# Planning the order of instructions with a transfer's issue and its bytes as two resources

## The chip, the cores and the metric
The kernel runs on one core of one Trainium2 chip. Its engines are TensorE (PE in the profile; PEld are its weight loads), VectorE (DVE), ScalarE (ACT), GpSimd (POOL) and SyncE (SP); here SP issues all transfers (DMAs). The metric is the device time of one execution in microseconds. Three runs of the kernel before took 653.82, 656.34 and 656.34 us; the median is 656.34 us.

## The reference
Causal attention over 4 batches of 12 heads (448 positions, 64 features each) gives x; a gated MLP follows. Weights arrive as 64-bit floats, and the kernel turns them into 32-bit ones.

```python
scores = scale * np.matmul(q, k.transpose(0, 1, 3, 2))
scores = np.where(mask, -1000000000.0, scores)
attn = np.exp(scores - np.max(scores, axis=-1, keepdims=True))
attn = attn / (np.sum(attn, axis=-1, keepdims=True) + 1e-09)
x = np.matmul(attn, v)               # then (batch*seq, heads*features) = (1792, 768)
gate = 1.0 / (1.0 + np.exp(-(x @ w_gate)))
out = gate * (x @ w_val) @ w_out     # w_gate, w_val: 768 x 1536; w_out: 1536 x 768
```

## The kernel before
Heads are taken in 24 pairs, six to a batch; a batch's 448 tokens are one unit of the MLP. Units 0 and 1 run the MLP as it stands (line 600: three matmuls for each product, since weights and activations are each split into a high and a low half). Units 2 and 3 are done together by a Strassen-like scheme with seven products in place of eight (line 813). First comes an opening with the attention of batch 0, up to about 45 us; then attention is mixed into the MLP of units 0 and 1: batch 1 in the narrow form, and from about 220 to 395 us batches 2 and 3 in the wide form; from 417 us on the paired units run alone.

A narrow pair loads `raw` (q and k, line 257) and `vr` (v, line 263), makes scores on TensorE, exponentials on ScalarE, scales on GpSimd, transposes on TensorE, copies to `pt`, and multiplies with v (line 358). A wide pair does the transposition differently: VectorE transposes blocks of 32 into `room`, one 1 MB transfer writes them to a buffer `pd` in device memory (line 463), four transfers of 256 KB read them back with the blocks in their new places as `pt` (line 466), and line 483 multiplies with `vr`.

A weight of units 0 and 1 is handled by `weight`. For unit 0 the 768 KB of 64-bit words go to `room` (line 565), ScalarE and VectorE build the 32-bit words in `wr` (lines 569 to 573), which are also stored to `wdram` (line 576); for unit 1 `wr` is read back from there (line 578). ScalarE then rounds to `wh` (line 581), and VectorE or GpSimd takes the rest, `wl` (line 583). There are three buffers each of `wr`, `wh` and `wl`.

The order of all this is written by no hand. Every operation is entered in a `Plan` with its engine, a cost in us, what it reads and writes, perhaps a due time, and an `extra`: time that passes after its end until another engine may use the result. `order()` first carries due times back from users to makers, then simulates the engines: the engine that can start earliest takes, among its operations ready by then, the one with the earliest due time. The starts so found give the sequence in which the instructions are emitted. Only the sequence reaches the chip: each engine then runs its own queue in that order and waits for semaphores, whatever times the plan had. SP is an engine in this plan as the others are: before the change a transfer holds it for its bytes at 355 GB/s and 0.03 us, and its result counts as there 2.8 or 4.2 us later. Three costs of the plan around the change:

```python
act = lambda n, psum=0, acc=0: n / 1200 + (0.06 if psum else 0.09) + 0.1 * acc
dma = lambda b: b / 355e3 + 0.03
LAT, LOOK, SLACK = 0.04, 0.06, 0.2
```

Of the kernel before, what the change touches and what calls it, by code (L numbers as in the profile page):

```python
# [10 lines left out]
I32 = mybir.dt.int32  # L11
# [4 lines left out]
B, H, S, D = 4, 12, 448, 64  # L16
DM, DFF = 768, 1536
KD, KF = DM // 128, DFF // 128
# [19 lines left out]
EV = ((1, 3, 4), (0, 1, 2, 3, 4), (1, 3, 4), (1, 3, 4))  # L38
BUFS = dict(w64=3, wd=2, wr=3, ws=3, sm=4, raw=3, pt=3, gt=5, vr=2, st=4)
LAT, LOOK, SLACK = 0.04, 0.06, 0.2  # L40
AFTER = dict(DVE=0.09, ACT=0.1, PL=0.03)


# [34 lines left out]


class Op:  # L80
    __slots__ = ("eng", "cost", "fn", "due", "preds", "succs", "make", "left", "ready", "n", "extra", "after", "then", "lock")


class Plan:
# [14 lines left out]
    def op(self, eng, cost, fn, reads=(), writes=(), due=None, extra=0.0, lock=False):  # L99
        o = Op()  # L100
        o.lock = lock or eng == "PL"
        o.eng, o.cost, o.fn, o.due, o.extra = eng, cost, fn, due, extra + AFTER.get(eng, 0.0)
        o.n = len(self.ops)
        preds = set()
        o.make, o.after, o.then = [], [], []
        for b, *ks in writes:
            if not b.ops:
                o.make.append(b)
                if b.before is not None:
                    preds.update(b.before.ops)  # L110
                if b.prev is not None and b.prev.ops:
                    o.after.append(b.prev.ops[0])
            else:
                o.after.append(b.ops[0])
        for b, *ks in reads:
            for k in ks or (0,):
                preds.add(b.last[k])
                b.readers.setdefault(k, []).append(o)
            b.ops.append(o)
        for b, *ks in writes:  # L120
            for k in ks or (0,):
                if k in b.last:
                    preds.add(b.last[k])
                preds.update(b.readers.get(k, ()))
                b.last[k] = o
                b.readers[k] = []
            b.ops.append(o)
        preds.discard(o)
        o.preds = preds
        o.succs = []  # L130
        o.after = [q for q in set(o.after) if q not in preds]
        for q in preds:
            q.succs.append(o)
        for q in o.after:
            q.then.append(o)
        self.ops.append(o)
        return o
# [6 lines left out]

    def order(self):
        for o in reversed(self.ops):
            d = min((s.due - s.cost - SLACK for s in o.succs), default=1e9) - o.extra
            o.due = d if o.due is None else min(o.due, d)
        free = {}
        shared = 0.0  # L150
        queue = {}
        for o in self.ops:
            o.left = len(o.preds) + len(o.after)
            o.ready = 0.0
            queue.setdefault(o.eng, [])
            free[o.eng] = 0.0
            if not o.left:
                queue[o.eng].append(o)
        done = []
        while True:  # L160
            best = None
            for e, q in queue.items():
                if q:
                    t = max(free[e], min(o.ready for o in q))
                    if best is None or t < best[0]:
                        best = (t, e)
            if best is None:
                break
            t, e = best
            q = queue[e]  # L170
            o = min((o for o in q if o.ready <= t + LOOK), key=lambda o: (o.due, o.n))
            q.remove(o)
            start = max(t, o.ready, shared if o.lock else 0.0)
            end = start + o.cost
            if o.lock:
                shared = end
            free[e] = end
            done.append((start, o.n, o))
            for s in o.succs:
                s.left -= 1  # L180
                s.ready = max(s.ready, end + o.extra + (LAT if s.eng != e or e != "PE" else 0.0))
                if not s.left:
                    queue[s.eng].append(s)
            for s in o.then:
                s.left -= 1
                s.ready = max(s.ready, start)
                if not s.left:
                    queue[s.eng].append(s)
        assert len(done) == len(self.ops)
        done.sort(key=lambda x: x[:2])  # L190
        return [o for _, _, o in done]
# [3 lines left out]
def kernel(  # L195
# [7 lines left out]
    nc = tc.nc  # L203
    plan = Plan()
# [7 lines left out]

    dve = lambda n: 0.07 + n / 960
    act = lambda n, psum=0, acc=0: n / 1200 + (0.06 if psum else 0.09) + 0.1 * acc
    dma = lambda b: b / 355e3 + 0.03

    ident = new("ident", [128, 128], F32)
    mask = new("mask", [128, 4 * WQ], F32)
# [31 lines left out]
    def load(n):  # L250
        j = pairs[n]
        j["raw"] = r = new("raw", [128, 2 * S], F32, BUFS["raw"])
        halves_ = lambda x: x.rearrange("p (y n) -> p y n", y=2)
        cols = (0, 2 * QB, S) if n == 0 else (0, S)
        for e, (a, c) in enumerate(zip(cols, cols[1:])):
            keys_ = (e,) if n == 0 else (0, 1)
            plan.op("SP", dma(128 * 2 * (c - a) * 4), lambda a=a, c=c: nc.sync.dma_start(
                out=halves_(r.t)[:, :, a:c], in_=halves_(qkt[n])[:, :, a:c]), writes=[(r, *keys_)], extra=2.8)

    def load_v(n):  # L260
        j = pairs[n]
        j["vr"] = v = new("vr", [128, NB, 2, D], F32, BUFS["vr"])
        plan.op("SP", dma(128 * NB * 2 * D * 4), lambda: nc.sync.dma_start(
            out=v.t.rearrange("p c z d -> p (c z d)"), in_=vt[n]), writes=[(v,)], extra=2.8)

    def score(n, blocks, due):

# [177 lines left out]
    def shift(n):  # L445
# [3 lines left out]
        tb = part(4 * WC, n % 2)  # L449
        tv = lambda: tb.t.rearrange("p (r n) -> p r n", r=4)  # L450
        plan.op("PL", 0.2, lambda: nc.gpsimd.memset(tv()[:, 2:4, WC - 32:WC], 0.0), [], [(tb, "zero")])
        for z, i in [(z, i) for i in range(3) for z in range(2)] + [(0, 3)]:
            sm, o, c, at = j["sm"][z], woff(i), min(i + 1, 3), z * 192 + ioff(i) if i < 3 else 384
            r = [(sm, (i, z))] if i < 3 else [(sm, (i, 0), (i, 1))]
# [6 lines left out]
            [(j["sm"][0], (3, 0), (3, 1))], [(tb, "end")])  # L461
        pd = new("pd", [128, 4 * WC], F32, 2, bass.MemoryType.DRAM)
        plan.op("SP", dma(128 * 4 * WC * 4), lambda: nc.sync.dma_start(out=pd.t, in_=tb.t),
                [(tb, "zero", "end", *[(z, i) for z in range(2) for i in range(3)], (0, 3))], [(pd,)], extra=4.2)
        for r in range(4):
            plan.op("SP", dma(32 * 4 * WC * 4), lambda r=r: nc.sync.dma_start(  # L466
                out=pt.t[32 * r:32 * r + 32, :4 * WC].rearrange("p (a n) -> p a n", a=4),
                in_=pd.t.rearrange("(a p) (r n) -> r p a n", a=4, r=4)[r]), [(pd,)], [(pt, r)], extra=4.2)

    def wpv(n, due):  # L470
        j = pairs[n]
# [82 lines left out]
    def weight(p):  # L554
# [3 lines left out]
        if p < NP:  # L558
# [4 lines left out]
            ri = lambda: t.t.rearrange("p k m -> p (k m)").bitcast(I32)  # L563
            n = KD * 128
            o = plan.op("SP", dma(128 * n * 8), lambda: nc.sync.dma_start(
                out=q.t.bitcast(I32), in_=wp[p]), [], [(q,)], extra=4.2)
            if p >= EARLY:
                plan.behind(o, pairs[min(HP - 2, 1 + p)]["r"].ops[0])
            plan.op("ACT", act(n) + 0.1, lambda: nc.scalar.activation(
# [3 lines left out]
            plan.op("DVE", 0.87, lambda: nc.vector.scalar_tensor_tensor(  # L573
                out=ri(), in0=lo(), scalar=29, in1=ri(), op0=ALU.logical_shift_right, op1=ALU.bitwise_or),
                [(q,)], [(t,)], lock=True)
            plan.op("SP", dma(128 * n * 4), lambda: nc.sync.dma_start(out=wd.t, in_=t.t), [(t,)], [(wd,)], extra=4.2)
        else:
            plan.op("SP", dma(128 * KD * 128 * 4), lambda: nc.sync.dma_start(out=t.t, in_=wd.t), [(wd,)], [(t,)], extra=4.2)
        hi_ = new("wh", [128, KD, 128], F32R, BUFS["ws"])
        lo_ = new("wl", [128, KD, 128], F32R, BUFS["ws"])  # L580
        plan.op("ACT", act(768), lambda: nc.scalar.copy(hi_.t, t.t), [(t,)], [(hi_,)])  # L581
# [6 lines left out]
    def unit_items(u):  # L588
# [44 lines left out]
        def f_out(m, half, k, due):  # L633
# [9 lines left out]
            if c == KF - 1:  # L643
                o = new("gt", [128, S], F32, BUFS["gt"])
                plan.op("ACT", act(S, 1), lambda: nc.scalar.activation(
                    out=o.t, in_=ps.t[:, :S], func=ACTF.Copy, scale=0.5), [(ps,)], [(o,)])
                plan.op("SP", dma(128 * S * 4), lambda: nc.sync.dma_start(
                    out=out[m * 128:(m + 1) * 128, u * S:(u + 1) * S], in_=o.t), [(o,)], [], due + 10.0, extra=4.2)

        order = [(jj, gv, k) for jj in range(KF) for gv in range(2) for k in range(KD)]  # L650
        if u == 0:
# [74 lines left out]
    def pair_items():  # L726
# [11 lines left out]
        def fetch(src, p=None):  # L738
            p = p or take()
            plan.op("SP", dma(128 * KD * 128 * 4), lambda: nc.sync.dma_start(  # L740
                out=p.t, in_=src.t.rearrange("p k m -> p (k m)")), [(src,)], [(p, 0, 1)], extra=4.2)
            return p

        def cut(p, lo=0, n=2, vector=False):
# [45 lines left out]
        def out_sums(m):  # L790
# [9 lines left out]
            for p, x in ("5", a22), ("7", a21), ("6", a11), ("3", a12):  # L800
                d = sums[p, m] = new(f"sum{p}{m}", [128, KD, 128], F32, 1, bass.MemoryType.DRAM)
                plan.op("SP", dma(128 * KD * 128 * 4), lambda d=d, x=x: nc.sync.dma_start(
                    out=d.t.rearrange("p k m -> p (k m)"), in_=x.t), [(x, 0, 1)], [(d,)], extra=4.2)
            sums["1", m], sums["2", m], sums["4", m] = at(m, 0), at(m, 1), at(KH + m, 1)

        sums = {}
# [35 lines left out]

        def write(src, row, u):
            plan.op("SP", dma(128 * S * 4), lambda: nc.sync.dma_start(
                out=out[row * 128:(row + 1) * 128, u * S:(u + 1) * S], in_=src.at), [src.ref], [], st["now"] + 10.0, extra=4.2)

        def stage():

# [237 lines left out]
```

## Time and profile before

| | before |
|---|---|
| runs (us) | 656.34, 653.82, 656.34 |
| profiled execution (us) | 654.04 |
| its span, first to last instruction (us) | 652.3 |
| granted TensorE clock, mean | 0.994 of full speed |
| busy us: TensorE, VectorE, ScalarE, GpSimd | 642.1, 445.5, 359.4, 323.3 |
| moved by transfers | 137.15 MB, mean 210 GB/s |

Busy time is the union of an engine's instructions; matmuls overlap, so their mean duration is longer than the distance from one start to the next. A wait is idle time of an engine, put down to what ended it. Time on SP's queue is issue time and waiting; the bytes move afterwards, and "to landing" counts from the issue to the last byte.

### The profile page before, as it was taken

How to read it: one execution, taken by the hardware profiler on the slowest of the kernel's cores; microseconds unless marked ns; L12 is line 12 of the kernel's file. 1: busy time of each engine (PE TensorE's matmuls, PEld its weight loads, DVE VectorE, ACT ScalarE, POOL GpSimd, SP SyncE). 2: the span in 40 equal slices, each digit the busy share in tenths (PEclk: the TensorE clock that was granted, in tenths of full speed). 3: DMA queues.
4: the chain of work that ended last, by engine and by line, in shares of the span. 5: the costliest groups of instructions: out<-in, count | busy, mean ns of one | idle time of the engine just before them, and what ended most of it. 6: DMA issues, size and time to landing. Idle time of an engine off the chain costs nothing.

```text
span 652.3 us, 10853 instructions
## 1 busy us (share of the span) xinstructions
PE 642.1 (98%) x3726; PEld 539.9 (83%) x3726; DVE 445.5 (68%) x999; ACT 359.4 (55%) x815; POOL 323.3 (50%) x352
## 2 busy tenths in 40 slices
PE   6999999999999999999999999999999999999997
PEld 4566887888888778778787899999999999999997
DVE  4776987878774376556565975647764459999852
ACT  6887777767664456555465645443343434556520
POOL 3751653241520277577666766756665657700300
PEclk9899999999999999999999999999999999999999
DMA  7379599877886369998989895767532322344321
GB/s 269 120 243 327 193 305 324 264 262 260 275 295 227 118 216 270 296 303 258 280 277 293 242 308 186 227 243 242 178 114 78 114 76 73 121 134 152 98 80 70
DMA packets 46678, 137.15 MB, mean 210 GB/s; under 512 B 5152, under 2 KB 8736, under 8 KB 45088
## 3 DMA queue, kind: packets, MB, share of 16 engines
q1 hardware_dynamic: 46624, 136.47, 64.0%
q8 instruction: 29, 0.48, 0.3%
q14 instruction: 25, 0.20, 0.1%
HBM read 99.48 MB, written 36.96 MB: 209 GB/s over the span
## 4 chain that ended last, share of the span: by engine, by line
PE 95%; DMA 2%; ACT 2%; SPq 0%; DVE 0%; POOL 0%; issue 0%; DVEq 0%
PE m L600 40%; PE m L813 19%; PE s L813 10%; PE t L813 7%; PE t L334 4%; PE s L283 4%; PE m L358 3%; PE m L483 3%; PE s L405 3%; DMA raw<-in_qkt_dram 2%; ACT sm L300 1%; PE t L405 1%; PE s L358 1%; POOL wl L583 0%; SPq L466 0%; ACT sm L426 0%
## 5 line engine op out<-in xcount | busy, mean ns | idle before, releaser
L767 POOL TENSOR_TENSOR wl<-room,wh 128x384 fp32r<-128x384 f32 x84 | 96.7, 1174 | 55.2 <-ACT wh L766 55.0
L600 PE MATMUL m<-xh,wh 128*128 128x448 f32 x288 | 109.8, 381 | 0.0
L600 PE MATMUL m<-xh,wl 128*128 128x448 f32 x288 | 105.3, 365 | 0.0
L600 PE MATMUL m<-xl,wh 128*128 128x448 f32 x288 | 105.2, 365 | 0.0
L583 POOL TENSOR_TENSOR wl<-wr,wh 128x768 fp32r<-128x768 f32 x38 | 74.4, 1961 | 54.0 <-ACT wh L581 53.4
L321 POOL TENSOR_SCALAR sm<-sm,r 112x112 f32<-112x112 f32 (+1 forms) x92 | 62.6, 701 | 77.4 <-DVE r L308 71.4
L581 ACT CAST wh<-wr 128x768 fp32r<-128x768 f32 x72 | 59.6, 830 | 30.7 <-PE m L600 19.6
L600 PEld LDWEIGHTS m<-xh,wh 128*128 128x128 f32 x288 | 54.1, 188 | 20.3 <-issue 13.3
L766 ACT CAST wh<-room 128x384 fp32r<-128x384 f32 x84 | 39.6, 512 | 54.2 <-POOL wl L767 15.9
L426 ACT ACTIVATE sm<-sm,mn 128x128 f32<-128x128 f32 (+3 forms) x84 | 43.9, 524 | 43.3 <-DVE mn L420 43.3
L600 PEld LDWEIGHTS m<-xh,wl 128*128 128x128 f32 x288 | 54.1, 188 | 4.5
L600 PEld LDWEIGHTS m<-xl,wh 128*128 128x128 f32 x288 | 54.2, 188 | 3.7
L300 ACT ACTIVATE sm<-sm,mn 112x112 f32<-112x112 f32 (+3 forms) x96 | 49.8, 521 | 9.8 <-DVE mn L296 9.4
L600 PE MATMUL m<-gh,wh 128*128 128x448 f32 x144 | 53.9, 374 | 0.0
L441 POOL TENSOR_SCALAR sm<-sm,r 128x256 f32<-128x256 f32 (+3 forms) x84 | 42.7, 525 | 21.7 <-DVE r L436 12.4
L583 DVE TENSOR_TENSOR wl<-wr,wh 128x768 fp32r<-128x768 f32 x34 | 36.2, 1065 | 24.2 <-ACT wh L581 23.9
L600 PE MATMUL m<-gh,wl 128*128 128x448 f32 x144 | 52.6, 366 | 0.0
L600 PE MATMUL m<-gl,wh 128*128 128x448 f32 x144 | 52.6, 365 | 0.0
L455 DVE STREAM_TRANSPOSE room<-sm 128x384 f32<-128x384 f32 (+2 forms) x84 | 35.1, 448 | 19.1 <-POOL sm L441 17.9
L630 POOL TENSOR_TENSOR gl<-gt,gh 128x448 fp32r<-128x448 f32 x24 | 30.4, 1268 | 34.2 <-ACT gh L629 34.2
L813 PE MATMUL m<-pt,wh 128*128 128x448 f32 x150 | 44.7, 366 | 0.0
L420 DVE CUSTOM_DVE_ANT_0 sm<-s,mask 128x128 f32<-128x128 f32 (+1 forms) x72 | 29.2, 440 | 21.5 <-PE s L405 20.9
(165 smaller groups left out, 1488.9 us busy)
## 6 DMA issues: line engine op xcount, KB each, us to landing
room<-in_wp_dram SPq DMA_DIRECT2D x36, 768.0 KB, 6.6
wr<-wdram SPq DMA_DIRECT2D x45, 384.0 KB, 5.0
room<-wdram SPq DMA_DIRECT2D x45, 384.0 KB, 3.6
wdram<-wr SPq DMA_DIRECT2D x36, 384.0 KB, 7.1
pd<-room SPq DMA_DIRECT2D x12, 1024.0 KB, 6.9
pt<-pd SPq DMA_DIRECT2D x48, 256.0 KB, 5.7
raw<-in_qkt_dram SPq DMA_DIRECT2D x23, 448.0 KB, 6.2
vr<-in_vt_dram SPq DMA_DIRECT2D x24, 256.0 KB, 6.1
```

The source lines that it names most:

```text
L300: plan.op("ACT", act(ne, 0, 1) + 0.01, lambda z=z, sm=sm, i=i, ne=ne, off=off: nc.scalar.activation(out=sm.t[:QB, off:off + ne], in_=sm.t[ ...
L321: plan.op("PL", 0.24 + w / 1200, lambda args=args: nc.gpsimd.tensor_scalar(**args()), [(r_,)], [(sm, a)])
L426: plan.op("ACT", act(ne, 0, 1) + 0.01, lambda z=z, sm=sm, i=i, ne=ne, off=off: nc.scalar.activation(out=sm.t[:, off:off + ne], in_=sm.t[:, ...
L441: plan.op("PL", 0.24 + w / 1200, lambda sm=sm, i=i, o=o, w=w, z=z: nc.gpsimd.tensor_scalar(out=sm.t[:, o:o + w], in0=sm.t[:, o:o + w], sca ...
L455: plan.op("DVE", dve(128 * c) + 0.03, lambda sm=sm, i=i, o=o, c=c, at=at: nc.vector.transpose(out=tv()[:, :, at:at + 32 * c].rearrange("p ...
L581: plan.op("ACT", act(768), lambda: nc.scalar.copy(hi_.t, t.t), [(t,)], [(hi_,)])
L583: plan.op(eng, cost, lambda: at.tensor_tensor(out=lo_.t, in0=t.t, in1=hi_.t.bitcast(F32), op=ALU.subtract), [(t,), (hi_,)], [(lo_,)], lock ...
L600: nc.tensor.matmul(out=ps.t[:, :S], lhsT=a.t[:, k, :], rhs=b.t if isinstance(b, Buf) else b(), start=(first and z == 0), stop=(last and z ...
L630: plan.op("PL", 1.11, lambda: nc.gpsimd.tensor_tensor(out=gl.t[:, jj], in0=gg.t, in1=gh.t.bitcast(F32), op=ALU.subtract), [(gg,), (gh,)], ...
L766: plan.op("ACT", act(w), lambda: nc.scalar.copy(f(hi_.t), x()), [(src, at)], [(hi_, e)])
L767: plan.op("PL", 0.97, lambda: nc.gpsimd.tensor_tensor(out=f(lo_.t), in0=x(), in1=f(hi_.t).bitcast(F32), op=ALU.subtract), [(src, at), (hi_ ...
L813: nc.tensor.matmul(out=ps.t[:, :S], lhsT=a.t[:, kw, :], rhs=b.at, start=bool(first and z == 0), stop=bool(last and z == 2), skip_group_che ...
```

## The change
A transfer has two costs in the plan. SP is held for `ISSUE`, 0.4 us. The bytes go into a second resource, `moved`: a transfer's end is the later of its issue and of the end of the transfer before it, plus its bytes at 330 GB/s (`load`). SP may issue ahead of the bytes by at most `BACKLOG`, 2.0 us. The time after the last byte is 2.2 us for every transfer. Due times subtract the bytes as well.

```diff
+ISSUE, BACKLOG = 0.4, 2.0
...
     def op(self, eng, cost, fn, reads=(), writes=(), due=None, extra=0.0, lock=False):
         o = Op()
         o.lock = lock or eng == "PL"
+        o.load = cost if eng == "SP" else 0.0
+        cost = ISSUE if eng == "SP" else cost
...
         for o in reversed(self.ops):
-            d = min((s.due - s.cost - SLACK for s in o.succs), default=1e9) - o.extra
+            d = min((s.due - s.cost - SLACK for s in o.succs), default=1e9) - o.extra - o.load
...
-        shared = 0.0
+        shared = moved = 0.0
...
             free[e] = end
+            if e == "SP":
+                end = moved = max(end, moved) + o.load
+                free[e] = max(free[e], moved - BACKLOG)
...
-    dma = lambda b: b / 355e3 + 0.03
+    dma = lambda b: b / 330e3
...
-                out=halves_(r.t)[:, :, a:c], in_=halves_(qkt[n])[:, :, a:c]), writes=[(r, *keys_)], extra=2.8)
+                out=halves_(r.t)[:, :, a:c], in_=halves_(qkt[n])[:, :, a:c]), writes=[(r, *keys_)], extra=2.2)
...
-            out=v.t.rearrange("p c z d -> p (c z d)"), in_=vt[n]), writes=[(v,)], extra=2.8)
+            out=v.t.rearrange("p c z d -> p (c z d)"), in_=vt[n]), writes=[(v,)], extra=2.2)
...
-                [(tb, "zero", "end", *[(z, i) for z in range(2) for i in range(3)], (0, 3))], [(pd,)], extra=4.2)
+                [(tb, "zero", "end", *[(z, i) for z in range(2) for i in range(3)], (0, 3))], [(pd,)], extra=2.2)
...
```

All other transfers (lines 466, 565, 576, 578, 647, 740, 802, 844) change `extra` from 4.2 to 2.2 in the same way.

## Rows read from the trace of the kernel before

**Rows 1.** The page, busy time, share of the span and instructions of each engine.
```profile
PE 642.1 (98%) x3726; PEld 539.9 (83%) x3726; DVE 445.5 (68%) x999; ACT 359.4 (55%) x815; POOL 323.3 (50%) x352
```

**Rows 2.** What PE waited for: total us, times, longest.
```profile
PE s L283 <- DMA raw<-in_qkt_dram: 4.0, 1, 4.0
...
PE m L483 <- DMA raw<-in_qkt_dram: 1.0, 1, 1.0
```

**Rows 3.** Pieces of the chain of waits: start, length in us, what.
```profile
45.46 2.63 PE m L600 x12
...
330.41 1.93 PE m L483 x40
...
343.63 1.93 PE m L483 x40
...
370.10 1.93 PE m L483 x40
...
393.48 1.93 PE m L483 x40
395.41 22.08 PE m L600 x108
```

**Rows 4.** Windows: PE, PEld, DVE, ACT, POOL busy (count), PE clock, DMA share, GB/s.
```profile
265.00:395.00 130.00, 130.00 (x980) 106.99 (x978) 82.74 (x276) 70.61 (x180) 86.38 (x102) 1.00 0.92 285
...
546.00:571.00 25.00, 25.00 (x123) 22.75 (x122) 24.13 (x32) 11.37 (x23) 18.51 (x15) 1.00 0.41 127
```

**Rows 5.** Timeline of SP's queue ahead of the stall: start, length in us, line.
```profile
250.44 3.10 SPq L578 DMA_DIRECT2D wr<-wdram  x2
253.63 0.38 SPq L263 DMA_DIRECT2D vr<-in_vt_dram  x1
```

**Rows 6.** Line 466 in three windows: issues, first and last start; time to landing.
```profile
L466 SPq DMA_DIRECT2D pt<-pd x4: 382/422/430, 254.1 to 255.5; - x4
...
DMA to landing us min/median/max: 5.0/7.0/8.5
...
L466 SPq DMA_DIRECT2D pt<-pd x4: 319/423/429, 357.6 to 358.9; - x4
...
DMA to landing us min/median/max: 4.1/5.2/6.3
...
L466 SPq DMA_DIRECT2D pt<-pd x4: 318/422/432, 386.3 to 387.7; - x4
...
DMA to landing us min/median/max: 3.5/4.6/5.5
```

**Rows 7.** The page, groups of line 600: busy us, mean ns, then idle time before.
```profile
L600 PE MATMUL m<-xh,wh 128*128 128x448 f32 x288 | 109.8, 381 | 0.0
L600 PE MATMUL m<-xh,wl 128*128 128x448 f32 x288 | 105.3, 365 | 0.0
...
L600 PEld LDWEIGHTS m<-xh,wh 128*128 128x128 f32 x288 | 54.1, 188 | 20.3 <-issue 13.3
```

**Rows 8.** The page, DMA issues: count, KB each, median us to landing.
```profile
wr<-wdram SPq DMA_DIRECT2D x45, 384.0 KB, 5.0
...
pd<-room SPq DMA_DIRECT2D x12, 1024.0 KB, 6.9
```

**Rows 9.** What SP's queue waited for: total us, times, longest.
```profile
SPq L578 <- POOL wl L583: 73.7, 31, 5.5
...
SPq L466 <- DMA pd<-room: 13.2, 7, 5.5
```

**Rows 10.** Timelines of POOL and of PE at the thinnest cover.
```profile
400.21 5.98 POOL L583 TENSOR_TENSOR wl<-wr,wh 128x768 fp32r<-128x768 f32 x1 [4.10 <-ACT wh L581]
...
406.39 0.36 PE L600 MATMUL m<-gh,wh 128*128 128x448 f32 x1
```

**Rows 11.** Timeline of SP's queue in the opening.
```profile
7.57 0.33 SPq L257 DMA_DIRECT2D raw<-in_qkt_dram  x1
7.94 0.43 SPq L565 DMA_DIRECT2D room<-in_wp_dram  x1
```

More of the change, by code (lines that the diff above doesn't have):

```diff
@@ L80 @@
 class Op:
-    __slots__ = ("eng", "cost", "fn", "due", "preds", "succs", "make", "left", "ready", "n", "extra", "after", "then", "lock")
+    __slots__ = ("eng", "cost", "fn", "due", "preds", "succs", "make", "left", "ready", "n", "extra", "after", "then", "lock", "load")
 class Plan:
@@ L467, in shift @@
                 out=pt.t[32 * r:32 * r + 32, :4 * WC].rearrange("p (a n) -> p a n", a=4),
-                in_=pd.t.rearrange("(a p) (r n) -> r p a n", a=4, r=4)[r]), [(pd,)], [(pt, r)], extra=4.2)
+                in_=pd.t.rearrange("(a p) (r n) -> r p a n", a=4, r=4)[r]), [(pd,)], [(pt, r)], extra=2.2)
     def wpv(n, due):
@@ L565, in weight @@
             o = plan.op("SP", dma(128 * n * 8), lambda: nc.sync.dma_start(
-                out=q.t.bitcast(I32), in_=wp[p]), [], [(q,)], extra=4.2)
+                out=q.t.bitcast(I32), in_=wp[p]), [], [(q,)], extra=2.2)
             if p >= EARLY:
@@ L575, in weight @@
                 [(q,)], [(t,)], lock=True)
-            plan.op("SP", dma(128 * n * 4), lambda: nc.sync.dma_start(out=wd.t, in_=t.t), [(t,)], [(wd,)], extra=4.2)
+            plan.op("SP", dma(128 * n * 4), lambda: nc.sync.dma_start(out=wd.t, in_=t.t), [(t,)], [(wd,)], extra=2.2)
         else:
-            plan.op("SP", dma(128 * KD * 128 * 4), lambda: nc.sync.dma_start(out=t.t, in_=wd.t), [(wd,)], [(t,)], extra=4.2)
+            plan.op("SP", dma(128 * KD * 128 * 4), lambda: nc.sync.dma_start(out=t.t, in_=wd.t), [(wd,)], [(t,)], extra=2.2)
         hi_ = new("wh", [128, KD, 128], F32R, BUFS["ws"])
@@ L647, in f_out @@
                 plan.op("SP", dma(128 * S * 4), lambda: nc.sync.dma_start(
-                    out=out[m * 128:(m + 1) * 128, u * S:(u + 1) * S], in_=o.t), [(o,)], [], due + 10.0, extra=4.2)
+                    out=out[m * 128:(m + 1) * 128, u * S:(u + 1) * S], in_=o.t), [(o,)], [], due + 10.0, extra=2.2)
         order = [(jj, gv, k) for jj in range(KF) for gv in range(2) for k in range(KD)]
@@ L740, in fetch @@
             plan.op("SP", dma(128 * KD * 128 * 4), lambda: nc.sync.dma_start(
-                out=p.t, in_=src.t.rearrange("p k m -> p (k m)")), [(src,)], [(p, 0, 1)], extra=4.2)
+                out=p.t, in_=src.t.rearrange("p k m -> p (k m)")), [(src,)], [(p, 0, 1)], extra=2.2)
             return p
@@ L802, in out_sums @@
                 plan.op("SP", dma(128 * KD * 128 * 4), lambda d=d, x=x: nc.sync.dma_start(
-                    out=d.t.rearrange("p k m -> p (k m)"), in_=x.t), [(x, 0, 1)], [(d,)], extra=4.2)
+                    out=d.t.rearrange("p k m -> p (k m)"), in_=x.t), [(x, 0, 1)], [(d,)], extra=2.2)
             sums["1", m], sums["2", m], sums["4", m] = at(m, 0), at(m, 1), at(KH + m, 1)
@@ L844, in write @@
             plan.op("SP", dma(128 * S * 4), lambda: nc.sync.dma_start(
-                out=out[row * 128:(row + 1) * 128, u * S:(u + 1) * S], in_=src.at), [src.ref], [], st["now"] + 10.0, extra=4.2)
+                out=out[row * 128:(row + 1) * 128, u * S:(u + 1) * S], in_=src.at), [src.ref], [], st["now"] + 10.0, extra=2.2)
         def stage():
```

## The prediction
> **What bounds the kernel now.** I read the busy line first. TensorE (PE) is busy for 642.1 of 652.3 us, 98%; the next engine, VectorE, for 445.5 [rows 1]. A busy PE is not yet a PE without stalls, so the second view is what PE waited for: the two longest of its few are 4.0 us for the first input load at the very start, where there is no other work, and 1.0 us at one place in the middle, line 483; the others belong to softmax in the opening, and none is for a weight [rows 2]. The third view is the chain of waits. It runs along PE itself for long pieces, 108 matmuls in 22.08 us, so one starts every 204 ns [rows 3], and the window of 265 to 395 us shows PE busy for 130.00 of 130 us [rows 4]. So the order of the other queues matters only where it makes PE late.
>
> The busy line has one weak side. The Trainium skill (Perfetto Trace Analysis, section Identifying the Most-Contended Engine) calls matmul busy time a bad measure of headroom and takes weight loads instead. By that rule 83% leaves 17%, an estimate of about 110 us. Here the row of the chain decides: 204 ns apart with no wait between them, and a new order doesn't change what one matmul takes. I keep it as a rival with a small chance.
>
> What could a better order of transfers win? The middle stall is the one wait that a transfer makes after the opening. PE stood at line 483, the product with v of a wide pair, which needs four pt reads. The row names the raw load [rows 2], but that one lands later; the four pt reads were issued at 254.1 to 255.5 us, and 255.5 plus the longest landing time, 8.5 us, is 264.0 [rows 6], when the product started. Ahead of them the queue of SP held a wr load up to 253.5 and a vr load at 253.63 [rows 5]. Gain at most: 1.0 us. A second item is the price of alternating between attention and MLP work on PE. The first matmul group of each triple takes 381 ns in the mean where the second takes 365, 16 ns on 288 [rows 7]: 4.6 us in all, to be saved only if PE alternates less.
>
> **The change, part by part.** No transfer, byte or instruction is added or removed; what changes is the planner's prices, and with them the sequence in each engine's queue. On the chip every queue then runs as fast as its waits allow, so a wrong price costs only where it puts a late instruction ahead of a ready one.
>
> (1) Time until data are usable. Worked out from the two codes for an idle queue, from the planned start of the issue: a 384 KB wr load goes from 1.14+4.2 = 5.3 us to 0.4+1.19+2.2 = 3.8; a 448 KB raw load from 4.1 to 4.0; the 1 MB pd write from 2.98+4.2 = 7.2 to 0.4+3.18+2.2 = 5.8; the last of four pt reads from 4x0.77+4.2 = 7.3 to 0.4+4x0.79+2.2 = 5.8. On a full queue the new plan adds up to its backlog, 2.0 us. The trace has medians of 5.0 for wr and 6.9 for pd [rows 8], and, from the first issue to the last landing of a pt group, 255.5+8.5-254.1 = 9.9, 358.9+6.3-357.6 = 7.6 and 387.7+5.5-386.3 = 6.9 [rows 6]. So pd and pt together, 14.5 us in the old plan and 11.6 to 15.6 in the new one, take 14 to 17. The old plan was about right for an idle queue here, the new one is right only with its backlog. For wr the measured 5.0 lies inside the new 3.8 to 5.8.
>
> What does that do to PE's own order? PE takes the earliest due among the instructions that the plan holds ready. An earlier readiness changes its order only where the old plan held the product back, and the pieces of the chain show it at even distances in the middle of the stretch, 13.22 us from 330.41 to 343.63 [rows 3]: it sits at its due position. Cost 0; bounds -1.0 (the stall above goes) and the price of the slower rival below.
>
> (2) Order on SP. The queue waits for most of its entries: 73.7 us in 31 waits for GpSimd to free a weight buffer (wr), up to 5.5 us each, and 13.2 us in 7 waits for pd to land [rows 9]. A pt group planned earlier moves ahead of a wr load; then the wr load and the vr and raw loads behind it wait for pd instead, at most the 5.5 us seen for one such wait. ScalarE, which rounds the weight, and GpSimd, which takes the rest, stand behind that load, and PE behind both. PE never waited for a weight [rows 2], and the cover is thinnest where the loads are scarce: the weight whose subtraction ends at 400.21+5.98 = 406.19 is used from 406.39 on, 0.2 us later [rows 10]. I take 0 for the wide stretch, because the chip's transfers there overlap anyway, and +0.3 for this near miss, between 0 and +3 (ScalarE must wait some microseconds more than the 0.2).
>
> (3) The opening. The second weight load stood behind the fourth raw load, which waited for its buffer until 7.57, and went out at 7.94 [rows 11]. In the new plan the queue is free for it before that buffer is (a load holds the queue for 0.4 us and not for its bytes), so it goes about 3 us earlier. Attention needs neither transfer then; PE takes its first weight only at 45.46 us [rows 3]. Its conversion on ScalarE could fall between two exponentials, at most one instruction late. Between -0.5 and +1, taken as 0.
>
> (4) Due times. Backward, the last pt read must now start 3.0 us before the product and not 4.2, and the steps that feed pd have dues about 3 us nearer to it (mostly 0.4 for pd's own place where 2.98 stood). A weight's load has its due 0.8 us nearer. This is a change of priority, felt only where two ready instructions want one engine: VectorE is busy 82.7, ScalarE 70.6, GpSimd 86.4 of 130 us [rows 4], so at least a third of each is free. Taken as 0; the bound is the slower rival.
>
> Sum against the profiled execution's own 654.04 us (span 652.3 and 1.74 around it): I count half of the 1.0 us stall as won, and 0.3 for the near miss as lost, -0.2, rounded up to -0.5 for a pair or two more of alternations saved: 653.5 us. The median of the three runs is 656.34, 2.3 above that execution, so the same change gives 655.8 us.
>
> **The rivals.**
> *Slower: pt late in the wide stretch.* By (4) the feeding chain may come up to 3 us later and still be planned in time. The data land 0.3 us before the product at the end (387.7+5.5 = 393.2 against 393.48), and 4.9 at the widest (358.9+6.3 = 365.2 against 370.10) [rows 3, 6]. With spare times spread evenly over 0 to 4.9, a chain 3 us late uncovers 3x3/(2x4.9) = 0.9 us for each of twelve pairs, 11 us; since every stall also gives the next pair more time, about half of that: 656.3+5.5 = 661.8. It decides once the delay passes about 1.7 us in the mean, where the loss (12x1.7x1.7/9.8 = 3.5) reaches 0.5%. For it: the spare time is small, and pd and pt are the slowest transfers against the new price. Against it: the planner starts what is ready and doesn't wait for a due, and the engines have idle time. Chance 0.16.
> *Slower, small: the handover at 546 to 571 us*, where VectorE is busy 24.13 of 25 us [rows 4], so any change of order there is felt: one instruction late, 1 to 2 us, 657.8. Chance 0.08; mostly within 0.5%.
> *Faster: PE alternates less.* If two thirds of the 4.6 us and the stall go, 656.3-4.1 = 652.2. For it: readiness is earlier everywhere. Against it: the alternation follows due times, which this change leaves to PE's own entries. Chance 0.07.
> *The order hardly moves.* Prices for raw and vr change by 0.1 to 0.2 us, and the queue order is set mostly by when buffers come free [rows 9]: 656.3. Chance 0.10.
> *PE isn't the bound.* If matmuls could close up from 204 ns to 188, the mean of one weight load [rows 7], 16 ns on 2430 would give 39 us, 617. It needs a stall that no view shows. This is the rule of the skill named above. Chance 0.01.
> The forecast itself has 0.58.
>
> **How the numbers follow.** Runs of this kernel lie up to 2.5 us apart, so about 0.5% (3.3 us) can be told from no change. Faster by more: 0.05 of the alternation rival, 0.01 of the last, 0.04 of the forecast, 0.10. Slower by more: 0.13 of the pt rival, 0.02 of the handover, 0.02 of the forecast and the unmoved order, 0.17. The rest, 0.73, is no difference. The forecast's own range is 654 to 657.5; to leave out no more than 2 in 10 it reaches down to 652.5 and up to 660.5, short of the pt rival's middle.
>
> **What would show it.** Right: PE's waits in the new profile again come to a few us, with 4.0 at the start, the product's starts stay some 13 us apart, and the chain stays on PE. The new order would show as pt reads issued right behind the landing of pd, more of SP's waits for pd and fewer for GpSimd ahead of them, and the second weight load before the fourth raw load. Wrong: several waits of 1 us or more at line 483 or on weights (the slower rivals), or long matmul runs that the old profile doesn't have and a busy line that is shorter by more than 3 us (the faster one).

## The result and the profile after

| | before | after |
|---|---|---|
| median of nine runs each, same chip (us) | 654.07 (653.26 to 656.34) | 659.48 (658.15 to 661.08) |
| ratio, 95% interval | 1 | 1.0081 [1.0068, 1.0094] |
| profiled execution: its time, its span | 654.04, 652.3 | 659.63, 657.9 |

The changed kernel is 5.4 us slower, 0.8%. The forecast was 655.8, a change too small to tell; 659.5 lies inside its range and on the other side of no change. In the ratios below, one run of e2_last (899 us, at a granted clock of 0.655) is left out. The kernel runs the same instructions as before. In the busy line and the groups of line 606 (600 before) nothing is dearer by more than 0.5%, against [rows 1, 7]: a matmul takes what it took, and PE alternates no less. First the busy line (busy time, share of the span, instructions), then two groups (busy, mean ns, idle before), all from the page of the kernel after:

```profile
PE 643.7 (98%) x3726; PEld 541.2 (82%) x3726; DVE 447.4 (68%) x999; ACT 358.3 (54%) x815; POOL 322.6 (49%) x352
...
L606 PE MATMUL m<-xh,wh 128*128 128x448 f32 x288 | 110.2, 382 | 0.0
L606 PE MATMUL m<-xh,wl 128*128 128x448 f32 x288 | 105.3, 366 | 0.0
```

What PE waited for (total, times, longest; the letter behind PE is the tile written) shows two waits that [rows 2] doesn't have, one for a weight and one for pt reads, and lacks the old 1.0 us at line 483:

```profile
PE s L289 <- DMA raw<-in_qkt_dram: 3.9, 1, 3.9
PE m L606 <- POOL wl L589: 2.1, 1, 2.1
PE m L489 <- DMA pt<-pd: 2.0, 1, 2.0
PE s L289 <- DVE mn L302: 1.0, 1, 1.0
PE t L340 <- ACT pt L349: 0.6, 1, 0.6
PE m L819 <- DVE xl L688: 0.4, 1, 0.4
```

Both stand in one place. The windows that answer [rows 4] (columns as there) lose PE time at the end of the first stretch and in the 15 us behind it; the handover at 546 us is as full as before:

```profile
265.00:395.00 130.00, 127.97 (x960) 105.11 (x962) 84.79 (x278) 69.39 (x179) 86.36 (x102) 1.00 0.87 278
395.00:410.00 15.00, 12.88 (x89) 11.52 (x86) 8.46 (x16) 6.58 (x12) 8.27 (x2) 1.00 0.37 139
546.00:571.00 25.00, 25.00 (x125) 23.01 (x124) 24.02 (x33) 12.46 (x27) 19.52 (x16) 1.00 0.31 96
```

The chain of waits of the kernel after from 380 to 410 us (start, length, what) tells the story in order, and answers the last pieces of [rows 3]:

```profile
379.46 7.67 DMA pd<-room
...
388.46 5.86 DMA pt<-pd
394.32 0.09 issue
394.41 2.00 PE m L489 x40
396.41 5.78 PE m L606 x27
402.19 0.03 POOLq L589
402.22 4.92 POOL wl L589
407.14 0.04 issue
407.18 2.90 PE m L606 x13
```

The last wide pair's pt reads landed some 1.2 us later than before (388.46+5.86 = 394.32; in [rows 6] 387.7+5.5 = 393.2), most of it because pd's write ahead of them took 7.67 us in place of 6.9. And PE was ready for the product at 392.4 and not at 393.4: its timeline, with the idle time in brackets.

```profile
392.01 0.37 PE L606 MATMUL m<-gh,wl 128*128 128x448 f32 x1
394.41 2.00 PE L489 MATMUL m<-pt,vr 128*64 128x128 f32 x40 [2.03 <-DMA pt<-pd]
```

The planner's own figures, from running the two kernels' `order()`, say why. "Ready" and "due" are the plan's times, in the order in which PE gets these entries; an MLP entry is three matmuls.

```
before   MLP, old weight   ready 386.65  due 368.4
         MLP, old weight   ready 387.26  due 369.2
         MLP, old weight   ready 387.86  due 370.0
         product           ready 389.15  due 368.2
         MLP, next weight  ready 389.15  due 368.4
after    product           ready 386.83  due 368.2
         MLP, old weight   ready 387.48  due 368.4
         MLP, next weight  ready 387.48  due 368.4
         MLP, old weight   ready 390.09  due 369.2
         MLP, next weight  ready 390.70  due 369.3
         MLP, old weight   ready 391.31  due 370.0
```

The plan is late here (ready lies some 20 us behind due), so an entry goes when it is ready. Of the attention entries of the wide stretch from 240 us on, this product is the only one that starts in the old plan when it becomes ready; the others are ready 1.2 to 4.2 us ahead. Before, the product was held back until its data counted as landed, and three entries of the old weight went first. With the shorter price it counts as landed 2.3 us earlier and stands nine matmuls earlier (9 x 0.205 = 1.8 us). Of the 0.3 us of spare time, 1.8 go for the matmuls and 1.2 for the landing, and 0.7 come back because this trace is that much late here: -2.0, the wait. Behind it the old weight's entries alternate with the next one's, so the old weight's last use, and with it its buffer, is later by the product (2.0), the wait (2.0) and six more matmuls (1.2).

The buffer's next weight shows the second stall. ScalarE rounds it at 399.75, GpSimd takes 6.48 us for its subtraction where the mean of line 589 is 1982 ns, and VectorE works without a gap until 405.47. Timelines of ScalarE, GpSimd and VectorE after:

```profile
396.44 0.53 ACT L373 COPY xl<-m 128x448 f32<-128x448 f32 x1 [5.17 <-PE m L489]
396.87 1.97 ACT L693 CAST pt<-xl 128x448 fp32r<-128x448 f32 x4
...
399.75 0.83 ACT L587 CAST wh<-wr 128x768 fp32r<-128x768 f32 x1
...
400.65 6.48 POOL L589 TENSOR_TENSOR wl<-wr,wh 128x768 fp32r<-128x768 f32 x1 [7.47 <-ACT wh L587]
...
397.01 0.63 DVE L688 TENSOR_TENSOR xl<-xl,xl 128x448 f32<-128x448 f32 x1 [8.43 <-ACT xl L373]
...
404.30 0.63 DVE L688 TENSOR_TENSOR xh<-xh,xl 128x448 f32<-128x448 f32 x1
404.84 0.63 DVE L698 TENSOR_TENSOR vr<-xl,pt 128x448 fp32r<-128x448 f32 x1
```

Before, the weight rounded ahead of the product was done in time, and the slow subtraction fell to a later one, which just arrived [rows 10]. The Trainium skill (SBUF — State Buffer, section Who interferes with whom) has a rule for the 6.48 us: a VectorE instruction with two inputs in SBUF and a GpSimd instruction that reads SBUF exclude each other, and whichever is first keeps the other out. The trace agrees: GpSimd's subtraction ends at 400.65+6.48 = 407.13, 1.7 us after the last instruction of VectorE's run, which is about the 1.8 us of an undisturbed one.

Where the 5.6 us of the spans go, by comparing the start of each n-th matmul in the two traces: +1.75 by 23 us, -1.1 at 264, +2.2 at the product, +2.45 at the weight, +0.6 near 460 us, -0.4 behind: 5.5. The first of these goes with the granted clock: it is 1.2 GHz for 10.2 us in the opening here and for 6.8 us in the trace before (last section), and 3.4 us at half the clock are an estimated 1.7 us of PE's work.

### The profile page after: what moved, and what is told of

Its sections match the earlier page's. It is cut to its first block, busy times and chain, and to the rows that moved or that the text cites. A ratio compares the mean times of both kernels' runs of the same rounds, so it can differ in the third digit from the quotient of the medians.

```text
span 657.9 us, 10854 instructions
## 1 busy us (share of the span) xinstructions
PE 643.7 (98%) x3726; PEld 541.2 (82%) x3726; DVE 447.4 (68%) x999; ACT 358.3 (54%) x815; POOL 322.6 (49%) x352
## 4 chain that ended last, share of the span: by engine, by line
PE 93%; DMA 3%; ACT 1%; DVE 1%; POOL 1%; issue 0%; SPq 0%; POOLq 0%; DVEq 0%
PE m L606 39%; PE m L819 18%; PE s L819 10%; PE t L819 6%; PE t L340 4%; PE s L289 4%; PE m L364 3%; PE m L489 3%; PE s L411 3%; ACT sm L306 1%; PE t L411 1%; DMA pd<-room 1%; DMA pt<-pd 1%; POOL wl L589 1%; PE s L364 1%
## 5 line engine op out<-in xcount | busy, mean ns | idle before, releaser
L589 POOL TENSOR_TENSOR wl<-wr,wh 128x768 fp32r<-128x768 f32 x38 | 75.3, 1982 | 59.2 <-ACT wh L587 58.6
L327 POOL TENSOR_SCALAR sm<-sm,r 112x112 f32<-112x112 f32 (+1 forms) x92 | 61.0, 683 | 84.9 <-DVE r L314 59.0
L589 DVE TENSOR_TENSOR wl<-wr,wh 128x768 fp32r<-128x768 f32 x34 | 38.5, 1132 | 25.6 <-ACT wh L587 25.4
L447 POOL TENSOR_SCALAR sm<-sm,r 128x256 f32<-128x256 f32 (+3 forms) x84 | 41.2, 506 | 22.2 <-DVE r L442 13.0
L575 ACT ACTIVATE wd<-room 128x768 f32<-128x768 f32 x36 | 32.9, 915 | 19.4 <-DMA room<-in_wp_dram 17.8
```

Source lines behind the costliest of these rows:

```text
L327: plan.op("PL", 0.24 + w / 1200, lambda args=args: nc.gpsimd.tensor_scalar(**args()), [(r_,)], [(sm, a)])
L447: plan.op("PL", 0.24 + w / 1200, lambda sm=sm, i=i, o=o, w=w, z=z: nc.gpsimd.tensor_scalar(out=sm.t[:, o:o + w], in0=sm.t[:, o:o + w], sca ...
L575: plan.op("ACT", act(n) + 0.1, lambda: nc.scalar.activation(out=d.t.bitcast(F32), in_=hi().bitcast(F32), func=ACTF.Prelu, scale=REBIAS, al ...
L589: plan.op(eng, cost, lambda: at.tensor_tensor(out=lo_.t, in0=t.t, in1=hi_.t.bitcast(F32), op=ALU.subtract), [(t,), (hi_,)], [(lo_,)], lock ...
```

## The experiments

The theory: the product's early place costs both waits. Rivals: the fetches that moved on SP, the opening, the two resources as such, and the clock. Ratios are to the kernel before, run beside; "last pair" is the last wide one.

**e1_open.** The opening's first two weight loads priced dearer, in the kernel after.

```diff
-                in_=wp[p]), [], [(q,)], extra=2.2)
+                in_=wp[p]), [], [(q,)], extra=3.2 if p < EARLY else 2.2)
```

> The changed kernel, with one price undone in part: the first two weight loads (768 KB each, in the opening) count as landed 1.0 us later in the plan (extra 3.2 in place of 2.2). In the order so written VectorE and ScalarE copy pt of the first pair before they convert these weights, as in the kernel before; after the opening the order is that of the changed kernel. Theory A (three places where PE comes late, each for itself): the 1.75 us lost by 23 us into the span go, 657.7 us against 659.5, and the two later stalls (2.0 us at 392, 2.1 us at 405) stay. Rival B (the traffic on SP's queue as a whole is what costs): the opening's transfers are the same, 659.5. Rival C (a lead in the opening is lost again at the next weight, because the weights are made no earlier): 659.5, with the lag back by 75 us.

660.09 us, 1.0088 [1.0069, 1.0107]: no gain, so Theory A misses here, and restoring the first loads alone is worth nothing. The late part went another way than expected, too. The wait for pt at the product is 2.4 us, but none follows at a weight: just behind the wait the granted clock falls to 1.2 GHz for 3.4 us (395.8 to 399.2). First the product with its wait, then a window (columns as in [rows 4]):

```profile
394.50 2.45 PE L489 MATMUL m<-pt,vr 128*64 128x128 f32 x40 [2.43 <-DMA pt<-pd]
...
396.00:399.00 3.00, 3.00 (x24) 2.66 (x21) 1.44 (x3) 2.01 (x5) 0.00 (x0) 0.50 0.95 377
```

PE falls back by 4.0 us from 391 to 400 us, wait and clock together, and meets the weight when it is there. So the early product costs about the same by a different second term.

**e2_last.** The old, longer time for the last pair's reads alone, in the kernel after.

```diff
-                ... [(pd,)], [(pt, r)], extra=2.2)
+                ... [(pd,)], [(pt, r)], extra=4.2 if n == B * HP - 1 else 2.2)
```

> The changed kernel, with one price undone: the four pt reads of the last wide pair alone count as landed 2.0 us later in the plan (extra 4.2 in place of 2.2). PE's order then has the last product where the kernel before has it, nine matmuls later; on SP three weight fetches for the paired units still go ahead of the weight loads of unit 1, as in the changed kernel. Theory A (the earlier place of the product costs both stalls: PE waits for pt, and ScalarE's rounding of the next weight, which needs a buffer that PE now frees later, falls behind the product's own follow-up): both stalls go, 659.5 - 2.0 - 2.2 = 655.3 us. Rival B (the second stall comes from the fetches that went ahead on SP): only the first goes, 657.5, and the wait of about 2 us for a weight stays.

655.0 us, 1.0011 [0.9995, 1.0026]. What PE waited for in it:

```profile
PE s L289 <- DMA raw<-in_qkt_dram: 4.0, 1, 4.0
PE s L289 <- DVE mn L302: 0.7, 1, 0.7
PE t L340 <- ACT pt L349: 0.6, 1, 0.6
PE t L340 <- POOL sm L327: 0.5, 2, 0.3
PE m L489 <- DMA pt<-pd: 0.5, 1, 0.5
```

The wait for wl is gone and that for pt is 0.5: 0.70% of the 0.81% hang on one price at one of twelve pairs. The fetches for the paired units still go ahead of the weight loads there on SP, so that rival falls.

**e3_both.** The edits of e1 and e2 together.

> Both edits of the two runs before this one. Theory A: they add up, 659.5 - 1.75 - 4.2 = 653.5 us, 0.5 us under the kernel before, because the 1.0 us stall of before at 263 us stays away. Rival C (what is won in the opening is lost again): 655.3.

655.23 us, 1.0023 [1.0005, 1.0041]: no better than e2 alone, where Theory A had 653.5.

**e4_back.** In the kernel before, the shorter time for the last pair's reads alone.

```diff
-                ... [(pd,)], [(pt, r)], extra=4.2)
+                ... [(pd,)], [(pt, r)], extra=2.2 if n == B * HP - 1 else 4.2)
```

> The kernel before, with one number of the change: the four pt reads of the last wide pair count as landed 2.0 us earlier in the plan (extra 2.2 in place of 4.2), one queue for issue and bytes as it was. In PE's order the last product then stands three matmuls earlier, and on ScalarE the rounding of the next weight stands behind the product's follow-up; SP's order of fetches and weight loads there hardly moves. Theory A: PE waits 0.3 us for pt (three matmuls are 0.6 us, the spare time was 0.3) and about 2 us for the weight, so 2 to 2.5 us over the kernel before, 656.3 against 654.1. Rival B (SP's order makes the stall): no more than 0.3 us over it, 654.4.

654.61 us, 1.0008 [0.9994, 1.0021]: a miss, at the figure of Rival B; e2 above and e9 below decide against that rival. The product stands three matmuls ahead, as expected, where the changed kernel has nine; 0.4 us of idle time stand before it and none at a weight. With the smaller move the waits don't come. Here GpSimd was first and VectorE stood: two subtractions of GpSimd, and VectorE's beside them, which take some 0.6 us otherwise.

```profile
396.64 2.24 POOL L583 TENSOR_TENSOR wl<-wr,wh 128x768 fp32r<-128x768 f32 x1 [5.38 <-ACT wh L581]
399.12 1.94 POOL L583 TENSOR_TENSOR wl<-wr,wh 128x768 fp32r<-128x768 f32 x1 [0.24 <-ACT wh L581]
...
397.09 2.28 DVE L692 TENSOR_TENSOR sm<-xl,pt 128x448 fp32r<-128x448 f32 x1
399.29 2.26 DVE L682 TENSOR_TENSOR xh<-xh,xl 128x448 f32<-128x448 f32 x1
```

**e5_dve.** The late weight's subtraction on VectorE, in the kernel after.

```diff
-        eng, cost, at = ("DVE", 0.87, nc.vector) if EARLY <= p < NP else ("PL", 1.8, nc.gpsimd)
+        eng, cost, at = ("DVE", 0.87, nc.vector) if EARLY <= p < NP or p == 68 else ("PL", 1.8, nc.gpsimd)
```

> The changed kernel; for one weight (index 68, the one that PE waits for at 405 us) VectorE takes the rest wl in place of GpSimd. PE's and ScalarE's order there, the product nine matmuls early with it, stay. Theory D (the weight's buffer is late, and then GpSimd, which VectorE's run of tensor operations for the paired units slows, takes 4.9 us and more for a subtraction that takes 2.0 elsewhere): with VectorE, about 1.1 us after the rounding ends at 400.6, the weight is there at about 402, before PE asks for it at 404.9, so the second stall of 2.1 us goes and the first, for pt, stays: 657.3 us. Rival E (the late rounding alone makes the stall, and VectorE's own queue is as late): the stall stays within 0.5 us, 659.0.

656.28 us, 1.0043 [1.0026, 1.0061]. The wait for wl is gone, the one for pt stays (2.1 us). Against the 1.0081 of the kernel after, the second term by itself is 0.38%, 2.5 us.

**e6_number.** The kernel before, one queue and its 355 GB/s, with 2.2 us for every transfer in place of 2.8 and 4.2.

```diff
-                ... [(pd,)], [(pt, r)], extra=4.2)
+                ... [(pd,)], [(pt, r)], extra=2.2)
```

> The kernel before with one part of the change: the time after the last byte is 2.2 us for every transfer; one queue for issue and bytes at 355 GB/s, as before. PE's order has the last product at the early place of the changed kernel, nine matmuls ahead. Theory F (the shorter time after the last byte is what moves the product, and with it the time): two stalls of about 2 us around 392 and 405 us, 658 to 659.5. Rival G (the two resources do it): no such stalls, 654 to 655.

662.21 us, 1.0120 [1.0090, 1.0150], above the bracket. PE waited for wl 2.3, at line 813 1.0, and 0.9 before a product at each of two lines. Behind the wait for wl, which ends at 407.2 us, the granted clock falls again:

```profile
409.00:411.00 2.00, 2.00 (x7) 1.78 (x6) 0.00 (x0) 1.00 (x2) 0.09 (x1) 0.50 0.72 238
```

PE loses 1.7 us there beyond the wait, which with the 1.0 at line 813 makes up what lies over 659.5. The shorter time after the last byte needs no second resource to do harm.

**e7_two.** The reverse: two resources, with the old 2.8 and 4.2.

```diff
-                ... [(pd,)], [(pt, r)], extra=2.2)
+                ... [(pd,)], [(pt, r)], extra=4.2)
```

> The changed kernel with the old times after the last byte (2.8 and 4.2 us): the two resources, 0.4 us an issue, 2.0 us of backlog and 330 GB/s stay. PE's order has the last product where the kernel before has it. Theory F: no stall at 392 or 405 us, and a time near that of the kernel before, 654 to 656 (the opening's order differs a little, up to 1.5 us). Rival G: the stalls are there, 658 to 659.5.

658.1 us, 1.0073 [1.0046, 1.0100], where 654 to 656 was expected: a miss. Nothing stalls near 392 or 405 us; PE waits 1.4 us for VectorE's r at line 440 ahead of a product instead, 0.8 at line 819 and 0.5 at another product. So the old times are no cure as such: this plan put other things at the edge. The trace explains 2.5 us alone: its execution took 656.53 us, the runs up to 662.2, and no trace of a longer one was kept.

**e8_front.** e2, and 3.2 us for the opening's transfers (raw as below, vr and the first two weights in the same way), which gives PE before's order up to 38 us.

```diff
-                ... in_=halves_(qkt[n])[:, :, a:c]), writes=[(r, *keys_)], extra=2.2)
+                ... in_=halves_(qkt[n])[:, :, a:c]), writes=[(r, *keys_)], extra=3.2 if n < HP else 2.2)
```

> The changed kernel; the last pair's pt reads count 2.0 us later as in the second run, and the transfers of the opening (q, k and v of the first six pairs, the first two weights) 1.0 us later (extra 3.2). The order of the opening is then that of the kernel before on PE up to 38 us and nearly on the others. Theory A (the opening's loss, 1.5 us at 55 us in the runs with only part of it restored, is one of order): it goes, and with the 1.0 us stall at 263 us gone too the time is 653.3, some 1 us under the kernel before. Rival C (the loss comes back from 38 to 55 us whatever the order ahead): 655.

655.16 us, 1.0032 [1.0019, 1.0045]: no gain over e2. Restoring PE's order up to 38 us wins nothing; its entries from there to 71 us still stand as in the kernel after, and no run restored those alone.

**e9_force.** The kernel before, made to rank the product ahead of the old weight's entries.

```diff
+    plan.behind(plan.ops[1974], plan.ops[1918])
     order = plan.order()
```

> The kernel before, with its one queue, its prices and its due times; one line more gives the last wide pair's product a lower rank than the entries of the old weight, so that it stands nine matmuls earlier on TensorE, and the entries of the old and of the next weight alternate behind it, as in the changed kernel. Theory (the product's early place is the cause, whatever brought it there): TensorE waits for the pt reads 1.5 to 2.2 us near 392 us and for the subtraction wl 1.5 to 2.5 us near 405 us; the time is 3.0 to 4.6 us above the kernel before, ratio 1.0046 to 1.0070. Rival (the place alone does little, the changed kernel's SP queue is needed for the loss): at most 1 us above, ratio up to 1.0015.

660.28 us, 1.0076 [1.0049, 1.0104], a little above the bracket. With before's prices and nearly its SP order, PE waits as in the kernel after (pd's write took 7.9 us here, 6.9 in the old trace, hence 3.2):

```profile
PE m L483 <- DMA pt<-pd: 3.2, 1, 3.2
PE m L600 <- POOL wl L583: 2.3, 1, 2.3
```

The place alone, with what follows from it, makes a loss of the whole size. It isn't the opening's clock: at the same mean granted clock of 0.997 two of these runs took 657.5 and 657.7 us, and four of the kernel before beside them 653.2 to 654.1.

**e12_whole.** The same early product, but the old weight's three entries together behind it.

```diff
     order = plan.order()
+    product = plan.ops[1918]
+    order.remove(product)
+    order.insert(order.index(plan.ops[1974]), product)
```

> The kernel before with only the product moved nine matmuls earlier in the finished order; the old weight's three entries stay together right behind it, ahead of the next weight's. Their buffer is then free six matmuls (6 x 0.205 = 1.2 us) earlier than in the changed kernel. Theory (two terms: the wait for the reads, and the weight made late because its buffer is freed late by the alternating entries): the wait for the reads stays at 1.5 to 2.2 us, the wait for wl falls to 0 to 1.2 us; the time is 1.5 to 3.2 us above the kernel before, ratio 1.0023 to 1.0049. Rival (the weight is late because the product itself is late, not because of the alternation): both waits stay, ratio 1.0055 or more. Second rival (the wait for the reads is given back later): ratio under 1.001.

657.43 us, 1.0052 [1.0035, 1.0070], a little above the bracket; the waits are in it:

```profile
PE m L483 <- DMA pt<-pd: 1.7, 1, 1.7
PE m L600 <- POOL wl L583: 1.3, 1, 1.3
```

The alternation is part of the second wait, not all of it: with it gone one weight is in time (398.14, 1.85 us) and the next meets VectorE (404.04, 5.94 us).

**e10_extra32.** The kernel after with 3.2 us for every transfer.

```diff
-                ... [(pd,)], [(pt, r)], extra=2.2)
+                ... [(pd,)], [(pt, r)], extra=3.2)
```

> The changed kernel with 3.2 us in place of 2.2 us from a transfer's last byte to the usable data, for every transfer: two resources kept, landings priced nearer to those measured. In the plan the product then stands behind the three entries of the old weight again. Theory (what costs is where single products and weights land in the order, not the two resources): neither wait near 392 and 405 us; 654 to 656 us, ratio to the kernel before 0.999 to 1.003. Rival (each new plan opens some stall of its own, because the plan's clock has little spare time): another wait of 1 to 2.5 us elsewhere, ratio 1.003 to 1.007. A truthful price making the kernel faster than before would show as a ratio under 0.9985.

656.8 us, 1.0050 [1.0031, 1.0068]. That is above what the theory expected and in the rival's bracket. The product stands behind the old weight's entries again and no wait over 0.3 us is left near 392 and 405. But its trace is 2.1 us late by 32 us, where the low clock lasts 10.2 us as in the kernel after, and 1.2 more by 55 us, 0.9 of it in one wait for GpSimd's scaling (line 327). A price nearer to the measured landings is better than 2.2 and still worse than the kernel before.

**e11_pt.** The kernel before, the four pt reads near 254 us ahead of the weight load and the vr load of [rows 5].

```diff
     order = plan.order()
+    pts = plan.ops[1154:1158]
+    order = [o for o in order if o not in pts]
+    at = order.index(plan.ops[1351])
+    order[at:at] = pts
```

> The kernel before with one change on SP: the four pt reads near 254 us are issued ahead of the weight load and the vr load that stood in front of them (the order of the changed kernel there). Theory: the only wait of TensorE there, 1.0 us for pt at 264 us, goes, and nothing else moves: 0.7 to 1.1 us less, ratio 0.9983 to 0.9990, at the edge of what the rounds can tell; the trace shows the wait gone. Rival: the weight load or vr, now behind four reads, is late in its turn (a wait of 0.5 us or more on wh, wl or vr near 262 to 268 us), ratio 0.9995 to 1.002.

653.32 us beside 653.57, 0.9986 [0.9972, 1.0000]. All that PE waits for in it, with no line 483:

```profile
PE s L283 <- DMA raw<-in_qkt_dram: 4.0, 1, 4.0
PE s L283 <- DVE mn L296: 0.7, 1, 0.7
PE t L334 <- POOL sm L321: 0.5, 2, 0.3
```

The 1.0 us wait is won, as sized in the prediction. It is the best version here, at the edge of what these runs tell.

## Why the prediction was wrong

That 659.5 lies inside the range is luck. The range was laid around 656.34, the median of three runs; nine runs have 654.07, and around that it would have ended at 658.2. The change in time was forecast as -0.5 and measured as +5.4 us. The prediction's own sign of being wrong is there: a wait of 2 us at line 489 (483 before) and one on a weight.

**The bound** was right: PE, 98% busy, and only its waits, with the clock in the opening and behind them, moved the time. "PE isn't the bound" fell with it, and "PE alternates less" too (382 ns against 381).

**Step (1) failed.** It said of the product: "it sits at its due position. Cost 0". That was read from even distances in the middle of the stretch. At its end the product sat where readiness put it, and the prediction had the sign of that before it: data that land 0.3 us before their use [rows 3, 6], where the widest pair has 4.9. This product had no spare time because it waited for its data in the plan too; with the shorter price it moved in front of them. Cost +2.2 us at the product and, by way of the weight behind it, +2.45 more, not 0. The same step had found that the new price is below the measured landings (5.8 us planned for four reads on an idle queue, 6.9 measured at this pair), and then did not ask which instruction that lets forward.

**Step (2), direction right, size wrong.** pt reads did move ahead of weight loads: SP's queue waited for pd 10 times, for GpSimd's release of a weight 21 times, against 7 and 31 in [rows 9].

```profile
SPq L584 <- POOL wl L589: 42.3, 21, 5.7
SPq L472 <- DMA pd<-room: 39.8, 10, 5.5
```

That cost nothing, as said. The near miss of 0.2 us was named, priced +0.3, and a weight there cost 2.45. That is inside its bound of +3; the value of +0.3 came from no row. The way it came about was another too: no load behind pt on SP, but a buffer held longer by PE's own order, and a GpSimd instruction that VectorE kept out. The row of 5.98 us against a mean of 2.0 for the same instruction was in front of the reader [rows 10] and was not asked why.

**The stall at 264 us** was counted as half won; it was wholly won. The four reads and the vr load behind them, on SP:

```profile
253.10 1.74 SPq L472 DMA_DIRECT2D pt<-pd  x4
254.94 0.38 SPq L269 DMA_DIRECT2D vr<-in_vt_dram  x1
```

**Step (3)**, the opening: the second weight load did not pass the fourth raw load (7.51 and 7.89 us, as in [rows 11]):

```profile
7.51 0.33 SPq L263 DMA_DIRECT2D raw<-in_qkt_dram  x1
7.89 0.43 SPq L571 DMA_DIRECT2D room<-in_wp_dram  x1
```

Its price of 0 is neither confirmed nor refuted. The trace after is 1.75 us late by 23 us, but traces there differ by that much with the clock (last section). e1, e3 and e8 moved the order there and won nothing. Still, e2 has the gain at 264 us in it, which e11 measures at 0.14%, and ends at 1.0011; some 0.25%, 1.6 us, of the changed plan remains unattributed. The traces put it ahead of 55 us: there, with 6.8 us of low clock each, e1, e2 and e3 are 1.4 to 1.6 us behind the kernel before, and e9, e11 and e12, which keep its order, 0.1 to 1.1. One profile each doesn't prove it. That stays open.

**Step (4)** and the rival drawn from it (a feeding chain that comes late at many pairs, 661.8 us) were wrong in kind: one pair of twelve stalled, mainly because its product went early: of the 3.0 us that ate its spare time 1.8 are the product's place and 1.2 the later landing. The loss of 5.4 us equals that rival's 5.5 by luck, from one place with two waits. At the handover ten of PE's entries changed places in the plan, and it cost nothing (-0.2 us).

## What to carry to other kernels

Where a planner writes the order, look for the instructions it holds back for data: here the one that started when it became ready had the least spare time on the chip, and the price that was too low put it ahead of its data. Price a near miss by what stands behind the late instruction (here a buffer, a rounding, a GpSimd instruction beside a busy VectorE, and in two traces the clock), and not by the delay that you expect. A plan that models a resource better isn't a better order: e10 and e7 keep the truer model and lose 0.5 and 0.7% at other places, while moving four reads by hand, where the trace shows a wait, takes that wait away and brings no other.

## What the hardware showed

GpSimd's subtraction takes 1.8 us alone and 6.48 beside a gapless run of VectorE instructions (5.4 to 6.5 in twelve of the fourteen traces, once in each); VectorE's take 2.3 in place of 0.6 when GpSimd was first (e4). What GpSimd lost was not one instruction's length but the whole run's.

The opening is run at either clock level. Windows of the kernel after, then of e4 (columns as in [rows 4]); the granted clock stands third from the end, 0.50 being 1.2 GHz and 1.00 being 2.4:

```profile
14.00:16.00 2.00, 1.72 (x7) 1.18 (x8) 1.80 (x5) 1.46 (x4) 1.18 (x3) 0.50 0.13 52
20.00:22.00 2.00, 2.00 (x10) 0.84 (x8) 1.64 (x2) 1.46 (x5) 1.33 (x2) 0.50 0.02 8
```

```profile
14.00:16.00 2.00, 1.26 (x8) 0.69 (x7) 1.54 (x5) 1.53 (x4) 1.79 (x4) 1.00 0.13 50
20.00:22.00 2.00, 2.00 (x17) 1.12 (x13) 2.00 (x7) 2.00 (x6) 1.84 (x3) 1.00 0.69 236
```

In the profiles of e4, e5 and e7 it stays at 1.00 throughout; in the others it is at 0.50 for 6.8 us between 12 and 24 us (10.2 in the kernel after, e8 and e10), ending near 20.5 us in the kernel before. From 12 to 14 us PE was busy 1.75 of the 2 us in the kernel after and 1.90 in e11, where the clock fell, and 1.86 in e5 and 1.41 in e7, where it stayed up: from this share one can't tell. By 265 us e4 is 1.5 us ahead of the kernel before although PE's order is the same up to there. So the first 24 us of a single profile say little about an edit here. The runs show the price: of those of the kernel before beside e1 to e4, 18 had a mean granted clock of 0.995 and a median of 654.6 us, and four had 1.00 and 652.1.

A wait can bring the low clock too, as behind the 2.4 us in e1 and the 2.3 us in e6. The kernels after, e1, e6 and e9, which all have the early product and GpSimd on the late weight, show a mean granted clock of 0.992 or less in 17 of 27 runs, the kernel before in none of the 78 beside the experiments. So part of their loss is the clock's: an estimated 1 us in the kernel after, whose two runs at 0.995 and 0.996 took 658.9 and 658.2 us against its median of 659.5. Which of them lost it in the opening and which behind a wait only a trace tells.
